# Late rows' scatters paced by the experts' products, result rows behind them, six result tiles

## The chip, the cores and the metric

One core of one Trainium2 chip. Its engines run side by side, each in the order of its own queue: PE multiplies (its products land in PSUM, in banks), DVE and ACT copy and compute, POOL here prepares and issues the indirect DMAs (scatters of rows to numbered places in DRAM), SP issues the other DMAs. They wait for each other by semaphores. The metric is the device time of the whole program in microseconds; lower is better.

## The reference, cut to what matters

```python
def reference(**kwargs):
    attn_out = _attn_ref(**attn_kwargs)            # (4, 4, 1088, 32)
    x = attn_out.transpose(0, 2, 1, 3).reshape(4352, 128)
    ...
    expert_idx = token_ids * np.int64(2654435761) % np.int64(8)
    for e in range(8):
        mask = expert_idx == e
        xe = x[mask]
        h = np.maximum(xe @ w1[e], 0.0)            # 128 -> 1024
        out[mask] = h @ w2[e]                      # 1024 -> 128
```

The attention (`_attn_ref`) is linear: features of q and k are products of two sketches, kv and z are sums over the sequence, and each of the 4352 rows of x is a quotient. All is float32.

## The kernel before, in words

**Attention.** Four batches go one after the other. Each ends in 8 blocks of 128 finished rows (`xs[b]`, b from 0 to 3); the last 64 rows of each batch are gathered in two tail tiles (`xs_tail`). A finished block is scattered to the DRAM table `x_rows`, where every expert has its own stretch: one indirect DMA of POOL per block, in `scatter_x` (line 686 in the profile). Batches 0 and 1 and the first tail are the early rows (8 + 8 + 1 scatters); they fill the experts' first 256 places. Batches 2 and 3 and the second tail are the late rows (17 scatters), which fill the places behind.

**Experts.** There are 16 groups: groups 0 to 7 are the first 256 rows of the 8 experts, groups 8 to 15 their late rows, between 313 and 278 each. A group has eight products of `layer1` (line 989, 128 of the 1024 hidden columns each, into a PSUM bank `hp`; four banks take turns), whose result ACT and DVE copy out through a ReLU in turn (`evict`, lines 774 and 776), and eight products of `layer2` (line 997, into `op`). The loop over (g, c) writes `layer1(g, c)`, then `layer2(g - 1, c)`, then what the table `beside` holds for that place. I call the place (g, c) slot 8g + c. The order on every engine is the order in which this program text is run; an instruction waits only for the data that it uses, and where `add_manual_dep` adds a wait.

**Rows in and out.** `fetch(k)` (SP, line 837) reads chunk k of `x_rows` from group k - 3 on; the chunks of groups 0 to 7 don't wait for the late rows, chunk 8 and later do. `turn_in` and `join_in` transpose it by DMA as two halves and put these together for `layer1`. On the way out, `out_columns` copies `op` as two halves (ACT), `turn_out` transposes them by two DMAs (SP, slot 8g + 1), `join_out` joins them in a tile `os` (DVE, slot 8g + 5), and `scatter_next` takes the next finished block of 128 rows and scatters it to the output (POOL, line 1000). `load_next` fetches the weights of experts 4 to 7, each load waiting for the product of its slot.

**What stands around the change.** `late_rows`, at slot 7, finishes the late rows' numbers (`sidx`, DVE) and then writes all 17 scatters, one right after the other. From group 2 on, `scatter_next` stands at c = 6, c = 7 and the next group's c = 0. `os` has three buffers, so the fourth `join_out` waits until the first tile's scatters have landed.

Of the kernel before, what the change touches and what calls it, by code (L numbers as in the profile page):

```python
# [9 lines left out]
F32 = mybir.dt.float32  # L10
# [14 lines left out]
def _half(ap, x):  # L25

    return ap.bitcast(U16).rearrange("p (n two) -> p n two", two=2)[:, :, x]
# [3 lines left out]
def kernel(  # L31
# [13 lines left out]
    P = 128  # L45
    B, H, S, D = q.shape
    R = S1.shape[0]
    N, DM = out.shape
    E, _, F = moe_w1.shape
    assert (H * D, DM, B * S, R * R * 2) == (P, P, N, P)  # L50
    T = S // P
    SM = T * P
    SP = S - SM
    TT = B // 2
# [5 lines left out]
    FC = F // P  # L60
# [6 lines left out]
    G = 2 * E  # L67
# [7 lines left out]
    XR = GE + N  # L75
    GQ = T // Q
    BIG = 1 << 30
    assert GE % P == 0 and caps[-1] >= P and ST <= P and 2 * CE == C and EB == TT


# [34 lines left out]
    def tail_col(cls):  # L115
        return cls * CE + TT * T

    def col_of(b, t):
        return b // TT * CE + b % TT * T + t
# [121 lines left out]
    G_.memset(empty_row[:], 0.0)  # L241
    G_.memset(empty_row[:, DM:DM + 1].bitcast(I32), BIG)

# [14 lines left out]
    xs = [const.tile([P, T, XW], F32, name=f"xs{b}") for b in range(B)]  # L258
    xs_tail = [const.tile([P, XW], F32, name=f"xs_tail{u}") for u in range(B // TT)]
# [218 lines left out]
    def route_blocks_end(p):  # L478
        own = spread[:].rearrange("p (n t) i -> p n t i", t=Q)
        nc.vector.tensor_tensor(own, p[:], own_t[:].unsqueeze(1).unsqueeze(3).to_broadcast([P, TT * GQ, Q, Q]), op=OP.mult)  # L480
        with nc.allow_low_precision(reason="the numbers of rows are whole"):
            to = sidx[:, main_cols(1)].rearrange("p (b i g) -> p b g i", b=TT, g=GQ)
            for b in range(TT):
                nc.vector.tensor_reduce(to[:, b], own[:, b * GQ:(b + 1) * GQ].rearrange("p g t i -> p g i t"), axis=AX.X, op=OP.add)
# [200 lines left out]
    def scatter_x(row, c):  # L685
        st_ = G_.indirect_dma_start(  # L686
            out=x_dram[:], out_offset=bass.IndirectOffsetOnAxis(ap=sidx[:, c:c + 1], axis=0),
            in_=row, in_offset=None, bounds_check=E * XR, oob_is_err=False)
        tc.declare_no_dep(st_.ins, group="x_rows", reason="distinct rows")
        tc.add_to_no_dep_group("x_rows", st_.ins)  # L690
        if c >= CE:
            tc.declare_no_dep(st_.ins, group="early_loads", reason="rows of late slots")
            tc.add_to_no_dep_group("late_rows", st_.ins)

    def x_tail(u, fT, psum=x_bank):
        p = x_tail_products(u, fT, ms[u * TT:(u + 1) * TT], psum)
        den = const.tile([P, 1, H], F32, tag="den_tail", name="den_tail", bufs=1)
        dens_of(den, [p], [(0, 1)])
        nc.vector.reciprocal(den[:], den[:])
        over_dens(xs_tail[u][:, 0:DM].unsqueeze(1), p, den[:], 1)  # L700

    def scatter_tail(u):
        scatter_x(xs_tail[u][:], tail_col(u))


    def side_turned(src):
# [74 lines left out]
    def first_of(g):  # L781
        if g <= E:
            return g * GE
        return E * GE + sum(caps[:g - E]) + (GAP if g >= G - 1 else 0)
# [25 lines left out]
    CT = 3  # L810
# [166 lines left out]
    moe = ctx.enter_context(tc.tile_pool(name="moe", bufs=3))  # L977
# [4 lines left out]
    last_mm = [None]  # L982
# [70 lines left out]

    def join_out():
        i, n, tts = turned_out.pop()
        os = moe.tile([P, CT, DM], F32, tag="os", name="os", bufs=3)
        for x in range(2):
            nc.vector.tensor_copy(_half(os[:].rearrange("p a b -> p (a b)"), x)[:, 0:n * DM],  # L1058
                                  tts[x][:, 0:n].rearrange("p a b -> p (a b)"))
        ready.extend((os[:, j], put[:, i + j:i + j + 1]) for j in range(n))  # L1060

    def out_rows(i, n):
        tp = ps_x.tile([P, CT, P], F32, tag="x", name="tp")
        for j in range(n):
            nc.tensor.transpose(tp[:, j], late_cols[:, (i + j) * P - LATE:(i + j + 1) * P - LATE], ident[:])
        os = moe.tile([P, CT, DM], F32, tag="os", name="os", bufs=3)
        for j in range(n):
            nc.vector.tensor_copy(os[:, j], tp[:, j])
        ready.extend((os[:, j], put[:, i + j:i + j + 1]) for j in range(n))
# [10 lines left out]
    def overflow_tables():  # L1080
        nc.vector.tensor_scalar(few[:], free_to[:, 1, E - 1:E], float(P), None, op0=OP.is_le)
        nc.vector.tensor_scalar(begin[:], place[:], -float(GD), float(GL + GE), op0=OP.mult, op1=OP.add)
        yield
        nc.vector.tensor_tensor(begin[:], begin[:], few[:].to_broadcast([P, E]), op=OP.mult)
        nc.vector.tensor_tensor(nt[:], left[:], begin[:], op=OP.subtract)
        yield
        nc.vector.tensor_scalar(nt[:], nt[:], float(GE + P - 1), 0.0, op0=OP.add, op1=OP.max)
        nc.vector.tensor_copy(nt_i[:], nt[:])
        yield
        nc.vector.tensor_scalar(nt_i[:], nt_i[:], P.bit_length() - 1, None, op0=OP.logical_shift_right)  # L1090
        nc.vector.tensor_copy(nt[:], nt_i[:])
        yield
        nc.vector.tensor_tensor_scan(ends[:], ones[:, 0:E], nt[:], 0.0, op0=OP.mult, op1=OP.add)
        nc.vector.tensor_copy(n_over[:], ends[:, E - 1:E])
# [4 lines left out]
    def at(g, c, f, *a):  # L1099
        beside.setdefault((g, c), []).append(lambda: f(*a))  # L1100

    def slot(n):
        return n // FC, n % FC
# [2 lines left out]

    def late_rows():
        route_blocks_end(route_blocks(bank))
        for b in range(TT, B):
            for t in range(T):  # L1110
                scatter_x(xs[b][:, t], col_of(b, t))
        scatter_tail(1)

    at(0, 7, late_rows)


    for k in range(4, G):
# [20 lines left out]
    for g in range(2, G - 1):  # L1138
        at(g, 1, turn_out, first_of(g - 1) // P)
        at(g, 5, join_out)  # L1140
        for c in (6, 7):
            at(g, c, scatter_next)
        at(g + 1, 0, scatter_next)
        if g == G - 4:

            at(g, 7, nc.gpsimd.drain)
        if g == G - 3:
            at(g + 1, 0, nc.gpsimd.drain)
    tables = overflow_tables()
    for i in range(5):  # L1150
        at(G - 5 + i // 4, 2 * (i % 4), next, tables, None)
# [13 lines left out]
    g, lo = G - 1, size_of(G - 1) - P  # L1165
# [26 lines left out]
    op = ps_o.tile([P, DM], F32, tag="o", name="op_rows")  # L1192
    for c in range(FC):
        nc.tensor.matmul(op[:], hTs[g][:, c, lo:lo + P], w2[:, g % E, c], start=(c == 0), stop=(c == FC - 1))
    os = moe.tile([P, CT, DM], F32, tag="os", name="os", bufs=3)
    nc.scalar.copy(os[:, 0], op[:])
    scatter(os[:, 0], put[:, ST - 1:ST])
    ordered.close()
# [7 lines left out]
    with tc.If(turns > 0):  # L1206
        nc.gpsimd.drain()
        with tc.For_i(0, turns):
# [15 lines left out]
            at = moe.tile([P, 6], F32, tag="at", name="at", bufs=1)  # L1224
# [46 lines left out]
            op = ps_o.tile([P, DM], F32, tag="o", name="op")  # L1271
            for c in range(FC):
                nc.tensor.matmul(op[:], hr[:, c], wo[1][:, c * P:(c + 1) * P], start=(c == 0), stop=(c == FC - 1))
            os = moe.tile([P, CT, DM], F32, tag="os", name="os", bufs=3)
            nc.scalar.copy(os[:, 0], op[:])
            scatter(os[:, 0], put1[:])

# [29 lines left out]
```

## Time and profile before

| | |
|---|---|
| median of 3 runs | 211.09 us (211.08 to 211.7) |
| the profiled execution | 210.28 us |
| its span, first to last instruction | 208.6 us |
| PE busy | 181.0 us (87%) |
| DVE, ACT, POOL busy | 90.8, 66.0, 81.5 us |
| scatters of POOL | 35 to `x_rows`, 35 to the output, about 0.98 us each |

The page's second part divides the span into 40 slices of 5.2 us and gives each engine's busy share there in tenths; PEclk is the granted clock of PE in tenths of 2.4 GHz. A row of a timeline has the start, the time, engine and line, the operation with its tiles, and in brackets how long the engine stood idle before it and what ended that; "issue" and "remote" mean that the profile shows nothing it waited for.

### The profile page before, as it was taken

How to read it: one execution, taken by the hardware profiler on the slowest of the kernel's cores; microseconds unless marked ns; L12 is line 12 of the kernel's file. 1: busy time of each engine (PE TensorE's matmuls, PEld its weight loads, DVE VectorE, ACT ScalarE, POOL GpSimd, SP SyncE). 2: the span in 40 equal slices, each digit the busy share in tenths (PEclk: the TensorE clock that was granted, in tenths of full speed). 3: DMA queues.
4: the chain of work that ended last, by engine and by line, in shares of the span. 5: the costliest groups of instructions: out<-in, count | busy, mean ns of one | idle time of the engine just before them, and what ended most of it. 6: DMA issues, size and time to landing. Idle time of an engine off the chain costs nothing. (4 is left out here: it accounts for less than half of the span.)

```text
span 208.6 us, 4037 instructions
## 1 busy us (share of the span) xinstructions
PE 181.0 (87%) x1459; PEld 142.0 (68%) x1459; DVE 90.8 (44%) x287; ACT 66.0 (32%) x176; POOL 81.5 (39%) x128
## 2 busy tenths in 40 slices
PE   8999839945988998137999999999999999999981
PEld 2769329725947886025888888877777777777970
DVE  3785536627455640003144426444525635424320
ACT  2587604420542721003133233313223132231220
POOL 7755751472010177771132133033213123054742
PEclk9999955995899999955799999999999999999999
DMA  4999999310019469312555495844153142150100
GB/s 121 272 344 294 318 303 337 85 57 31 3 47 272 127 171 210 95 57 81 134 165 148 99 176 149 94 91 101 43 104 72 38 106 71 27 91 25 38 30 28
DMA packets 43524, 26.35 MB, mean 126 GB/s; under 512 B 21913, under 2 KB 41370, under 8 KB 43503
## 3 DMA queue, kind: packets, MB, share of 16 engines
q1 hardware_dynamic: 40383, 21.14, 40.3%
q0 software_dynamic: 2304, 4.78, 8.4%
q8 instruction: 12, 0.20, 0.4%
q10 hardware_dynamic: 816, 0.17, 0.4%
q14 instruction: 9, 0.07, 0.1%
HBM read 17.42 MB, written 4.95 MB: 107 GB/s over the span
## 5 line engine op out<-in xcount | busy, mean ns | idle before, releaser
L997 PE MATMUL op<-hT,w 128*128 128x256 f32 (+8 forms) x256 | 78.2, 397 | 0.0
L1000 POOL DMA_INDIRECT out_dram<-os,put x35 | 34.6, 989 | 77.8 <-DVE os L1058 61.7
L776 DVE TENSOR_SCALAR hT<-hp 128x256 f32<-128x256 f32 (+9 forms) x64 | 27.4, 428 | 77.4 <-PE hp L989 50.6
L997 PEld LDWEIGHTS op<-hT,w 128*128 128x128 f32 x256 | 48.8, 195 | 11.2
L774 ACT ACTIVATE hT<-hp 128x256 f32<-128x256 f32 (+9 forms) x72 | 27.9, 390 | 78.4 <-PE hp L989 59.2
L989 PE MATMUL hp<-xT,w 128*128 128x256 f32 x128 | 40.1, 404 | 9.7 <-issue 8.3
L989 PE MATMUL hp<-xT_late,w 128*128 128x313 f32 (+8 forms) x144 | 41.9, 386 | 0.0
L686 POOL DMA_INDIRECT x_rows<-xs,sidx x32 | 31.5, 983 | 21.5 <-issue 8.5
L989 PEld LDWEIGHTS hp<-xT,w 128*128 128x128 f32 x128 | 24.9, 200 | 15.4 <-issue 9.9
L989 PEld LDWEIGHTS hp<-xT_late,w 128*128 128x128 f32 x144 | 25.3, 189 | 7.0 <-issue 0.3
L622 PE MATMUL kv<-va,kp 128*64 128x33 f32 x256 | 12.9, 247 | 9.6 <-issue 9.4
L622 PEld LDWEIGHTS kv<-va,kp 128*64 128x64 f32 x256 | 11.6, 165 | 13.7 <-issue 11.9
L560 DVE TENSOR_TENSOR fT<-q_first,each_ps 128x512 f32<-128x512 f32 x16 | 10.4, 684 | 14.3 <-remote 11.7
L544 PE MATMUL each_ps<-qT,s_each 32*64 32x512 f32 x128 | 12.4, 609 | 1.1 <-ACT q_first L556 0.7
L556 ACT COPY q_first<-each_ps 128x512 f32<-128x512 f32 x16 | 8.9, 593 | 4.4 <-PE each_ps L544 3.6
L644 PE MATMUL x_ps<-m,fT 128*64 128x66 f32 x256 | 9.0, 230 | 0.5 <-ACT m L631 0.5
L644 PEld LDWEIGHTS x_ps<-m,fT 128*64 128x64 f32 x256 | 8.4, 144 | 1.3 <-ACT m L631 0.6
L865 DVE COPY xh<-xg 128x256 uint16<-128x256 uint16 (+1 forms) x28 | 8.4, 340 | 0.0
L631 ACT COPY m<-kv 64x66 f32<-64x66 f32 x8 | 1.7, 209 | 19.8 <-PE kv L622 19.8
L544 PEld LDWEIGHTS each_ps<-qT,s_each 32*64 32x64 f32 x128 | 3.9, 130 | 5.8 <-ACT q_first L556 3.0
L1037 ACT COPY half<-op 128x256 uint16<-128x256 uint16 x16 | 5.2, 377 | 6.5 <-PE op L997 5.5
L1058 DVE COPY os<-turned 128x256 uint16<-128x256 uint16 (+1 forms) x26 | 6.8, 311 | 0.6 <-DMA turned<-half 0.6
(170 smaller groups left out, 138.3 us busy)
## 6 DMA issues: line engine op xcount, KB each, us to landing
w<-in_moe_w_dram SPq DMA_DIRECT2D x16, 512.0 KB
q<-in_q_dram SPq DMA_DIRECT2D x4, 512.0 KB
v<-in_v_dram SPq DMA_DIRECT2D x4, 512.0 KB
xg<-x_rows SPq DMA_DIRECT2D x12, 129.0 KB
k<-in_k_dram SPq DMA_DIRECT2D x3, 512.0 KB
out_dram<-os,put POOLq DMA_INDIRECT x35
x_rows<-xs,sidx POOLq DMA_INDIRECT x32
k<-in_k_dram SPq DMA_DIRECT2D x3, 128.0 KB
```

The lines of the kernel that those rows point to most:

```text
L544: nc.tensor.matmul(p[HALVES[x]], s_each[rows, a].rearrange("p i j -> p (i j)"), src_of(rows, x), start=True, stop=True, skip_group_check=True)
L556: nc.scalar.copy(firsts[:, t], ps[t][:])
L560: nc.vector.tensor_tensor(fT[:, t * GQ:(t + 1) * GQ], firsts[:, t], ps[t][:], op=OP.mult)
L622: nc.tensor.matmul(kv[HALVES[x], z], f[:, x], w[:, x], start=(n == 0 and z == 0), stop=(n == T), skip_group_check=True)
L644: nc.tensor.matmul(p[x, j, z], fT[:, t0 + j, z, x], m[:, z], start=True, stop=True, skip_group_check=True)
L686: st_ = G_.indirect_dma_start(out=x_dram[:], out_offset=bass.IndirectOffsetOnAxis(ap=sidx[:, c:c + 1], axis=0), in_=row, in_offset=None, b ...
L774: nc.scalar.activation(dst, src, AF.Relu if relu else AF.Copy)
L776: return nc.vector.tensor_scalar(dst, src, 0.0, None, op0=OP.max).ins
L865: nc.vector.tensor_copy(xh[:, x * w:(x + 1) * w].rearrange("p (a b) -> p a b", a=n), xg3[k][:, 0:n].bitcast(U16).rearrange("p a (b two) -> ...
L989: last_mm[0] = nc.tensor.matmul(hp[:, 0:hi - lo], w1[:, g % E, c * P:(c + 1) * P], x_columns(first_of(g) + lo, first_of(g) + hi), start=Tr ...
L997: nc.tensor.matmul(ops[g][:, 0:hi - lo], w2[:, g % E, c], hTs[g][:, c, lo:hi], start=(c == 0), stop=(c == FC - 1))
L1000: st_ = nc.gpsimd.indirect_dma_start(out=out[:], out_offset=bass.IndirectOffsetOnAxis(ap=idx, axis=0), in_=src, in_offset=None, bounds_che ...
```

## The change

`late_rows` now only prepares the 17 scatters. `late_next` writes one of them, and makes it wait for the layer1 product of the slot in which it stands (`beside_now`); it stands at slots 7, 9, 11, ..., 39. `scatter_next` no longer stands three times per group: it stands at every second slot from 41 to 119, and takes a block if one is finished in program order. It waits for no product. `os` gets six buffers.

```diff
+    OS = 6
...
-        os = moe.tile([P, CT, DM], F32, tag="os", name="os", bufs=3)
+        os = moe.tile([P, CT, DM], F32, tag="os", name="os", bufs=OS)
...
     def late_rows():
         route_blocks_end(route_blocks(bank))
-        for b in range(TT, B):
-            for t in range(T):
-                scatter_x(xs[b][:, t], col_of(b, t))
-        scatter_tail(1)
-
-    at(0, 7, late_rows)
+        late_rows_left.extend(lambda b=b, t=t: scatter_x(xs[b][:, t], col_of(b, t)) for b in range(TT, B) for t in range(T))
+        late_rows_left.append(lambda: scatter_tail(1))
+
+    late_rows_left = []
+
+    def beside_now(ins):
+        tc.add_manual_dep(ins, last_mm[0].ins.name,
+                          mybir.DependencyInfo(mybir.DependencyClass.Sync, mybir.DependencyReason.DATA), reason="pace")
+
+    def late_next():
+        beside_now(late_rows_left.pop(0)().ins)
+
+    LATE_AT = 7
+    at(*slot(LATE_AT), late_rows)
+    for i in range(2 * T + 1):
+        at(*slot(LATE_AT + 2 * i), late_next)
+    OUT_AT = LATE_AT + 2 * (2 * T + 1)
...
-        for c in (6, 7):
-            at(g, c, scatter_next)
-        at(g + 1, 0, scatter_next)
...
+    for i in range(OUT_AT, (G - 1) * FC, 2):
+        at(*slot(i), scatter_next)
```

The orders on PE and ACT are as they were, and so is SP's. On POOL the scatters keep their sequence; what differs is what they wait for. Here are the first late scatters on POOL before, in slot 7 (`xs2` is the tile of batch 2, `sidx` the row numbers; DMASW0 to DMASW7 are the semaphores of POOL's DMAs, used in turn, so that each scatter waits for the one eight before it; PE and DVE are those engines' own):

```order
L1021 MEMSET late_cols_1125 128x68 [waits DMAHW2_49,DMAHW3_49,DMAHW1_49,DMAHW5_49,DMAHW0_49,DMAHW6_49,DVE_49,DMAHW7_49,PE_49,Pool_49]
L686 DMA x_rows<-xs2_187,sidx_224 36993x144 [waits DMASW4_49,DVE_49]
L686 DMA x_rows<-xs2_187,sidx_224 36993x144 [waits DMASW5_49]
L686 DMA x_rows<-xs2_187,sidx_224 36993x144 [waits DMASW6_49]
L686 DMA x_rows<-xs2_187,sidx_224 36993x144 [waits DMASW7_49]
```

And the same place after:

```order
L1023 MEMSET late_cols_1125 128x68 [waits DMAHW2_49,DMAHW3_49,DMAHW1_49,DMAHW5_49,DMAHW0_49,DMAHW6_49,DVE_49,DMAHW7_49,PE_49,Pool_49]
L687 DMA x_rows<-xs2_187,sidx_224 36993x144 [waits DMASW4_49,DVE_49,PE_49]
L687 DMA x_rows<-xs2_187,sidx_224 36993x144 [waits DMASW5_49,PE_49]
L687 DMA x_rows<-xs2_187,sidx_224 36993x144 [waits DMASW6_49,PE_49]
L687 DMA x_rows<-xs2_187,sidx_224 36993x144 [waits DMASW7_49,PE_49]
```

Each late scatter has got a wait for PE, and nothing else has moved. The next place on POOL is the end of the late rows and the first result rows; before, the last four late scatters (`xs3`, `xs_tail1`) stand back to back in slot 7, the result rows in groups 2 to 4:

```order
L686 DMA x_rows<-xs3_188,sidx_224 36993x144 [waits DMASW1_49]
L686 DMA x_rows<-xs3_188,sidx_224 36993x144 [waits DMASW2_49]
L686 DMA x_rows<-xs3_188,sidx_224 36993x144 [waits DMASW3_49]
L686 DMA x_rows<-xs_tail1_190,sidx_224 36993x144 [waits DMASW4_49]
L1000 DMA out_0_dram<-os_1319,put_225 4352x128 [waits DMASW5_49,DVE_49]
L1000 DMA out_0_dram<-os_1319,put_225 4352x128 [waits DMASW6_49]
L1000 DMA out_0_dram<-os_1383,put_225 4352x128 [waits DMASW7_49,DVE_49]
L1000 DMA out_0_dram<-os_1383,put_225 4352x128 [waits DMASW0_49]
L1000 DMA out_0_dram<-os_1445,put_225 4352x128 [waits DMASW1_49,DVE_49]
L1000 DMA out_0_dram<-os_1445,put_225 4352x128 [waits DMASW2_49]
```

After, with the late scatters at slots 33 to 39 and the result rows from slot 41 on:

```order
L687 DMA x_rows<-xs3_188,sidx_224 36993x144 [waits DMASW1_49,PE_49]
L687 DMA x_rows<-xs3_188,sidx_224 36993x144 [waits DMASW2_49,PE_49]
L687 DMA x_rows<-xs3_188,sidx_224 36993x144 [waits DMASW3_49,PE_49]
L687 DMA x_rows<-xs_tail1_190,sidx_224 36993x144 [waits DMASW4_49,PE_49]
L1002 DMA out_0_dram<-os_1292,put_225 4352x128 [waits DMASW5_49,DVE_49]
L1002 DMA out_0_dram<-os_1292,put_225 4352x128 [waits DMASW6_49]
L1002 DMA out_0_dram<-os_1362,put_225 4352x128 [waits DMASW7_49,DVE_49]
L1002 DMA out_0_dram<-os_1362,put_225 4352x128 [waits DMASW0_49]
L1002 DMA out_0_dram<-os_1430,put_225 4352x128 [waits DMASW1_49,DVE_49]
L1002 DMA out_0_dram<-os_1430,put_225 4352x128 [waits DMASW2_49]
```

The late ones wait for a product of PE; the result rows behind them wait for DVE's copies into their `os` tile and for no product, though they now stand from slot 41 on. The third place is DVE at the fourth `join_out` (slot 45), before:

```order
L776 TENSOR_SCALAR hT_1470<-hp_1492 128x256 [waits PE_49]
L776 TENSOR_SCALAR hT_1470<-hp_1504 128x256 [waits PE_49]
L872 COPY xT_1508<-xh_turned_1454 128x256 [waits DMAHW1_49]
L872 COPY xT_1508<-xh_turned_1454 128x256
L1058 COPY os_1511<-turned0_1480 128x256 [waits DMAHW2_49,DMASW6_49,DMASW5_49]
L1058 COPY os_1511<-turned1_1482 128x256 [waits DMAHW3_49]
L846 COPY put_225<-xg3_1428 128x2 [waits DMAHW7_49]
```

And after:

```order
L778 TENSOR_SCALAR hT_1452<-hp_1477 128x256 [waits PE_49]
L778 TENSOR_SCALAR hT_1452<-hp_1492 128x256 [waits PE_49]
L874 COPY xT_1496<-xh_turned_1439 128x256 [waits DMAHW1_49]
L874 COPY xT_1496<-xh_turned_1439 128x256
L1060 COPY os_1499<-turned0_1462 128x256 [waits DMAHW2_49]
L1060 COPY os_1499<-turned1_1464 128x256 [waits DMAHW3_49]
L848 COPY put_225<-xg3_1407 128x2 [waits DMAHW7_49]
```

The copy into the fourth `os` tile no longer waits for the two scatters (DMASW6, DMASW5) that empty the first tile.

## Rows read from the trace of the kernel before

**Rows 1.** The page: the span, and the busy share of PE in 40 slices of 5.2 us with its granted clock.

```profile
span 208.6 us, 4037 instructions
...
PE   8999839945988998137999999999999999999981
...
PEclk9999955995899999955799999999999999999999
```

**Rows 2.** The timeline of PE alone from 70 to 112 us: the layer1 products of slots 17 to 27 (the second of group 2 to the fourth of group 3); the rows left out between them are layer2's.

```profile
78.77 0.59 PE L989 MATMUL hp<-xT,w 128*128 128x256 f32 x2
...
79.64 0.59 PE L989 MATMUL hp<-xT,w 128*128 128x256 f32 x2
...
80.50 0.59 PE L989 MATMUL hp<-xT,w 128*128 128x256 f32 x2
...
81.36 0.59 PE L989 MATMUL hp<-xT,w 128*128 128x256 f32 x2
...
83.24 0.70 PE L989 MATMUL hp<-xT,w 128*128 128x256 f32 x2 [0.85 <-issue]
...
88.98 1.22 PE L989 MATMUL hp<-xT,w 128*128 128x256 f32 x2 [4.61 <-issue]
...
93.94 1.22 PE L989 MATMUL hp<-xT,w 128*128 128x256 f32 x2 [2.88 <-issue]
...
97.32 1.19 PE L989 MATMUL hp<-xT,w 128*128 128x256 f32 x2 [1.30 <-ACT half L1037]
...
99.16 1.06 PE L989 MATMUL hp<-xT,w 128*128 128x256 f32 x2
...
100.87 1.06 PE L989 MATMUL hp<-xT,w 128*128 128x256 f32 x2
...
102.20 0.59 PE L989 MATMUL hp<-xT,w 128*128 128x256 f32 x2
```

**Rows 3.** Busy time of the engines in three stretches: from and to, length, busy us and instructions of PE, PEld, DVE, ACT and POOL, granted clock, mean share of the 16 DMA engines, GB/s.

```profile
78.40:82.40 4.00, 3.99 (x19) 3.16 (x17) 0.00 (x0) 0.78 (x3) 3.08 (x4) 1.00 1.16 226
82.40:102.20 19.80, 10.16 (x25) 6.99 (x25) 3.31 (x12) 2.20 (x7) 10.56 (x11) 0.66 0.36 97
102.20:130.00 27.80, 27.80 (x130) 24.38 (x129) 12.52 (x44) 8.50 (x25) 7.97 (x8) 1.00 0.59 140
```

**Rows 4.** The timeline of ACT alone: its copies out of layer1's banks at slots 18 and 20 (the second row with slot 22 as well).

```profile
88.55 0.38 ACT L774 ACTIVATE hT<-hp 128x256 f32<-128x256 f32 x1 [9.15 <-remote]
96.29 0.66 ACT L774 ACTIVATE hT<-hp 128x256 f32<-128x256 f32 x2 [7.36 <-PE op L997]
```

**Rows 5.** The timeline of DVE alone: its copies out of the banks of slots 17, 19 and 21, then the first and the last of a block of copies once a group, the last being that of the next bank.

```profile
82.76 0.43 DVE L776 TENSOR_SCALAR hT<-hp 128x256 f32<-128x256 f32 x1 [4.66 <-PE op L997]
93.47 0.42 DVE L776 TENSOR_SCALAR hT<-hp 128x256 f32<-128x256 f32 x1 [10.28 <-issue]
96.37 0.43 DVE L776 TENSOR_SCALAR hT<-hp 128x256 f32<-128x256 f32 x1 [2.48 <-PE op L997]
96.72 0.50 DVE L872 COPY xT<-xh_turned 128x256 uint16<-128x256 uint16 x2
...
97.99 0.41 DVE L776 TENSOR_SCALAR hT<-hp 128x256 f32<-128x256 f32 x1
```

**Rows 6.** The timeline of POOL alone: the first and the last of the 17 late scatters.

```profile
71.89 0.98 POOL L686 DMA_INDIRECT x_rows<-xs,sidx  x1 [8.32 <-DVE sidx L484]
...
92.42 0.98 POOL L686 DMA_INDIRECT x_rows<-xs_tail,sidx  x1 [0.30 <-issue]
```

**Rows 7.** The same for the early rows: the first scatter of the first run of eight, the first of the second run of eight, and the first tail's scatter.

```profile
19.30 1.11 POOL L686 DMA_INDIRECT x_rows<-xs,sidx  x1 [1.48 <-DVE xs L663]
...
38.71 0.97 POOL L686 DMA_INDIRECT x_rows<-xs,sidx  x1 [2.91 <-DVE xs L663]
...
58.12 0.98 POOL L686 DMA_INDIRECT x_rows<-xs_tail,sidx  x1 [9.46 <-DVE xs_tail L663]
```

**Rows 8.** The timeline of PE alone in the attention: the rows from which on its products of kv follow each other without a gap again.

```profile
30.74 2.39 PE L622 MATMUL kv<-va,kp 128*64 128x33 f32 x41 [1.07 <-issue]
...
50.08 1.94 PE L622 MATMUL kv<-va,kp 128*64 128x33 f32 x32 [0.51 <-issue]
```

**Rows 9.** Busy time in three more stretches, columns as in rows 3: the two runs of eight, and 14 us of the experts with two pairs of result rows.

```profile
19.30:30.80 11.50, 7.01 (x74) 4.49 (x73) 5.69 (x10) 4.62 (x9) 7.99 (x8) 0.82 1.02 307
38.70:50.10 11.40, 6.38 (x81) 3.80 (x78) 5.35 (x10) 3.55 (x7) 7.82 (x8) 0.87 0.16 53
103.00:117.00 14.00, 14.00 (x67) 12.26 (x66) 6.14 (x23) 4.17 (x12) 4.01 (x4) 1.00 0.54 146
```

**Rows 10.** The timeline of SP's queue: the fetches of the first four chunks, a load of weights, the transposes of `turn_in` and `turn_out`, and the fetch of chunk 8.

```profile
60.63 1.91 SPq L837 DMA_DIRECT2D xg<-x_rows  x4
...
78.95 0.01 SPq L176 DMA_DIRECT2D w<-in_moe_w_dram  x1
79.69 0.81 SPq L867 DMA_TRANSPOSE xh_turned<-xh  x1
81.22 2.81 SPq L1050 DMA_TRANSPOSE turned<-half  x2
...
117.28 1.09 SPq L837 DMA_DIRECT2D xg<-x_rows  x3
```

More of the change, by code (lines that the diff above doesn't have):

```diff
@@ L693, in scatter_x @@
             tc.add_to_no_dep_group("late_rows", st_.ins)
+        return st_
     def x_tail(u, fT, psum=x_bank):
@@ L702, in scatter_tail @@
     def scatter_tail(u):
-        scatter_x(xs_tail[u][:], tail_col(u))
+        return scatter_x(xs_tail[u][:], tail_col(u))
     def side_turned(src):
@@ L1065, in out_rows @@
             nc.tensor.transpose(tp[:, j], late_cols[:, (i + j) * P - LATE:(i + j + 1) * P - LATE], ident[:])
-        os = moe.tile([P, CT, DM], F32, tag="os", name="os", bufs=3)
+        os = moe.tile([P, CT, DM], F32, tag="os", name="os", bufs=OS)
         for j in range(n):
@@ L1194 @@
         nc.tensor.matmul(op[:], hTs[g][:, c, lo:lo + P], w2[:, g % E, c], start=(c == 0), stop=(c == FC - 1))
-    os = moe.tile([P, CT, DM], F32, tag="os", name="os", bufs=3)
+    os = moe.tile([P, CT, DM], F32, tag="os", name="os", bufs=OS)
     nc.scalar.copy(os[:, 0], op[:])
@@ L1273 @@
                 nc.tensor.matmul(op[:], hr[:, c], wo[1][:, c * P:(c + 1) * P], start=(c == 0), stop=(c == FC - 1))
-            os = moe.tile([P, CT, DM], F32, tag="os", name="os", bufs=3)
+            os = moe.tile([P, CT, DM], F32, tag="os", name="os", bufs=OS)
             nc.scalar.copy(os[:, 0], op[:])
```

## The prediction

> **What bounds the kernel now.** I read the page first [rows 1]: PE is at nine tenths or more of almost every slice of the experts' half, except slices 17 to 19 (about 83 to 99 us), where it falls to 1, 3 and 7 tenths and its clock to half. Then the timeline of PE through that hole [rows 2]. I count slots: slot n is the n-th product of layer1, eight to a group, from group 1 on with one product of layer2 behind it; slot 17 is the second of group 2. Slots 17 to 20 start at 78.77, 79.64, 80.50 and 81.36, so a slot takes (81.36 - 78.77)/3 = 0.863 us. Slots 21, 22, 23 and 24 start at 83.24, 88.98, 93.94 and 97.32, slots 24 to 26 at half clock (about 1.71 us each), and from slot 27 (102.20) the pace is regular again. At the regular pace slot 27 would have started at 81.36 + 7 x 0.863 = 87.40. **The hole costs 102.20 - 87.40 = 14.8 us.** Behind it PE is busy 27.80 of 27.80 us [rows 3], so what is lost there is lost at the end.
>
> What is PE waiting for? Its four hp banks. Slot 21 needs the bank of slot 17, which DVE empties at 82.76 (0.43 us, and PE starts at 83.24); slot 22 needs that of slot 18, emptied by ACT at 88.55 (PE: 88.98); slot 23 that of slot 19, by DVE at 93.47 (PE: 93.94) [rows 2, 4, 5]. And ACT and DVE? They stand idle for 9.15 and 10.28 us in front of these copies, although the products were issued at 79.64 and 80.50. The products are long done; the word of it arrives late. At 96.29 and 96.37 both come free at once.
>
> What ends there? POOL's run of 17 late scatters, begun at 71.89 and issued every (92.42 - 71.89)/16 = 1.28 us [rows 6]. The two earlier runs of eight show the same: they begin at 19.30 and 38.71 [rows 7], PE crawls in pieces that wait for nothing the profile shows, and full speed is back at 30.74 and 50.08 [rows 8]. Per scatter, from the run's start to the release: (30.74 - 19.30)/8 = 1.43, (50.08 - 38.71)/8 = 1.42, (96.29 - 71.89)/17 = 1.435. Three runs of different length give one figure: behind POOL something serves a scatter in about 1.43 us, POOL feeds it one every 1.28, and while it is behind, PE's messages pass only now and then. Pairs of scatters do no harm: from 103 to 117, four scatters in two pairs, PE 14.00 of 14.00 [rows 9].
>
> **The change, part by part.** *Late rows spaced out.* The 17 scatters come at slots 7, 9, ... 39 and each waits for that slot's layer1 product. Two slots are 1.73 us, more than 1.43, so nothing builds up, with 0.30 us to spare per scatter. The first few are still fed every 1.28 us (the first cannot start before its row numbers, 71.89 now; by then slots 7 and 9 are issued), which is four scatters and no more. So the hole goes: -14.8 us. The wait feeds back the right way: if PE's word is late, the next scatter is late too. What is left is that one scatter may hold a message back for up to 1.43 us. A bank is needed again four slots later, 3.45 us, less 0.59 for the product and 0.43 for the copy: 2.4 us to spare; DVE's block of copies once a group (96.72 to 97.99 [rows 5]) eats 1.3 of it. I take 0.5 us for the whole stretch, between 0 and 2. Behind the waiting scatter on POOL stand only scatters. The waits cost no instruction on PE, whose order is untouched.
>
> *Late rows end later.* Slot 39 falls at 78.77 + 22 x 0.863 = 97.8; its product takes 0.59, so the last late scatter starts at about 98.3 instead of 92.42. The tail's scatter at 58.12 let the fetch behind it go at 60.63 [rows 7, 10], so issue to landing is 2.5 us: 100.8. Its first reader is the fetch of chunk 8 on SP at slot 42 (100.3). SP has two transposes of turn_out ahead of it at slot 41 (2.81 us for the pair at 81.22), so that it would not come before about 102.4 anyway; today it comes at 117.28, 2.1 us behind its slot [rows 10]. Cost 0. If that cover were gone, 0.5 us of SP would shift, with ten slots before group 7 needs what is queued behind it.
>
> The Trainium skill, "DMA: Bandwidth & Descriptors", section "Rules for kernel authors", speaks against this move: issue a DMA early and wait on its semaphore late. By that rule these scatters were best where they were; the landing above says that the last one still has 1.6 us in hand, so by the rule too the sum would lose nothing here.
>
> *Result rows behind them.* Now they go two per group from group 2 on, as soon as joined. After the change the first stands behind the last late scatter, and it waits for its os tile alone, not for PE. By then three os tiles (joined at slots 21, 29, 37) are full, six scatters, and the fourth (slot 45, about 102.9) is full before POOL gets to it at 98.3 + 7 x 1.28 = 107.3. So POOL issues nine in a row: the last late one and eight results. The fifth tile (slot 53, about 109.8, its copies a microsecond later) makes a pause. By 1.43 us per scatter the messages are free at 98.3 + 9 x 1.43 = 111.2. **This is the new wait.** Lower bound: nothing, since the experts' own run held PE up only from 82.4 on, 10.5 us after its start, and nine scatters last 12.9: 2.4 us. Upper bound: in the runs of eight PE idled 11.50 - 7.01 = 4.5 and 11.40 - 6.38 = 5.0 us [rows 9]; nine give 5.6, and if the clock falls behind that (it was 0.82 and 0.87 there), five slots at half clock, as many as in the hole (22 to 26), add 5 x 0.85 = 4.3: 9.9. The nearest row is that of the experts' own stretch; I take 3.
>
> *Six buffers.* Slot 45's join no longer waits for the first tile's two scatters; without the three more buffers it would wait for them to land at about 103.4, half a microsecond. Worth 0 beside the above. The last part of the kernel keeps its scatters.
>
> Sum: -14.8 + 0.5 + 3 = -11.3. The profiled execution took 210.28 us (span 208.6 and 1.7 around it), so 199.0; the median of the runs is 0.8 higher, so **199.8 us**.
>
> **The rivals.** *The result rows cost nothing* (nine scatters are too few to stop four banks): -14.8 to -13.3, about 197. For it: the 10.5 us of grace above. Against: the runs of eight. *They cost all they can*, with the clock: -14.8 + 0.5 + 5.6 to 9.9, about 202 to 207, in the middle 204.5. For it: both runs of eight lowered the clock. Against: PE's products were then small and far fewer.
>
> *The scatters are not the cause.* At 78.95 SP issues a load of weights, then three transposes [rows 10], and the DMA share is 1.16 from 78.4 to 82.4 [rows 3], just before the first late copy. If that holds PE up, the hole stays and so does the time, 211.1. Against: from 38.7 to 50.1 the share was 0.16 and PE idled all the same, and from 103 to 117 loads and transposes ran without harm [rows 9]. The Trainium skill, same page, section "Issuing engines are not separate DMA queues", says that DMAs of all issuers end on the same 16 engines and interleave; by that alone spreading them moves no work and the time stays 211.1. The 0.36 share in the hole [rows 3] says that these engines were not full.
>
> *Slower: single scatters are enough.* Each scatter may hold PE's messages for its own 1.43 of 1.73 us, DVE's block of copies takes the rest of the slack, PE waits a little in every slot and its clock falls to 1.2 GHz for the whole paced stretch, where a slot takes 1.71 instead of 0.863 us. For all 33 slots that is 27.9 us against the 14.8 saved: 211.1 + 13.1 = 224. It decides from 14.8/0.85 = 17 slots on. Against: at 1.71 us per slot a scatter comes every 3.4 us and the cause is gone; and in the present run PE still issued regularly at 81.36, 9.5 us in.
>
> **How the numbers follow.** Forecast 0.47; result rows free 0.25; result rows at full price 0.18; not the cause 0.04; slower 0.06. The range takes the first two whole and the near half of the third: 195.8 (all of the 14.8, and half a microsecond for the runs' own spread) to 205.5. About 0.3% is what a measurement of this kernel tells from no change: faster 0.90, within 0.3% 0.04, slower 0.06.
>
> **What would show it.** After: layer1 products 0.86 us apart from slot 17 to slot 38, x_rows scatters 1.73 us apart from the fifth on, no copy of ACT or DVE with more than 3 us of idle in front before about 103. A run of nine scatters from about 98, the last eight to out_dram, and any idle of PE between 103 and 112 released at its start + 9 x 1.43. The forecast is wrong if PE is regular through 112 (too slow by 3), if its clock falls there (too fast), or if copies come late while scatters are 1.73 us apart (the cause is misread). The fetch of chunk 8 should go at about 102.4 and wait for no x_rows.

## The result, and the profile after

| | before | after |
|---|---|---|
| median of 4 runs each | 211.17 us (211.08 to 211.7) | 201.81 us (201.36 to 204.26) |
| ratio, 95% interval | | 0.9575 (0.9496 to 0.9655): faster |
| the profiled execution, its span | 210.28, 208.6 us | 201.49, 199.6 us |

The forecast was 199.8 us, range 195.8 to 205.5. Single executions of one kernel lie up to 6 us apart (198.71 to 204.95 us for e4b_three_buffers below), so below I rest on stretches of a trace where I can, and on medians only for larger differences; ratios leave disturbed executions out, and so aren't always the quotient of the medians.

Four parts of the profile after answer to rows of before. First the page, as in [rows 1]:

```profile
span 199.6 us, 4046 instructions
...
PE   8989937982988999999998599999999999999970
...
PEclk9999995897599999999999799999999999999997
```

The 1, 3 and 7 of slices 17 to 19 are gone, and a new dip to 5 stands in slice 23 (about 110 to 115 us), with the clock at 7 in it. Next the timeline of PE, the products of layer1 at slots 9, 23, 24, 49, 50, 51, 52 and 54, which answers to [rows 2]:

```profile
72.20 0.59 PE L991 MATMUL hp<-xT,w 128*128 128x256 f32 x2
...
84.30 0.59 PE L991 MATMUL hp<-xT,w 128*128 128x256 f32 x2
...
85.40 0.67 PE L991 MATMUL hp<-xT,w 128*128 128x256 f32 x2
...
107.06 0.59 PE L991 MATMUL hp<-xT,w 128*128 128x256 f32 x2
...
108.46 0.70 PE L991 MATMUL hp<-xT,w 128*128 128x256 f32 x2 [0.37 <-ACT hT L776]
...
111.47 0.73 PE L991 MATMUL hp<-xT,w 128*128 128x256 f32 x2 [1.88 <-issue]
...
113.39 1.22 PE L991 MATMUL hp<-xT,w 128*128 128x256 f32 x2 [0.34 <-ACT hT L776]
...
116.21 0.59 PE L991 MATMUL hp<-xT,w 128*128 128x256 f32 x2
```

From slot 9 to slot 23 there are 14 slots in 84.30 - 72.20 = 12.10 us, 0.864 each. Slot 24 is (85.40 - 84.30) - 0.86 = 0.24 us late, and then all is regular up to slot 49. Slot 54 would come at 107.06 + 5 x 0.8635 = 111.38; it comes at 116.21. **The new loss is 4.83 us**: 2.59 us of idle in three gaps, the rest products at the lower clock (1.22 us for a pair at slot 52) and short waits. What ends it stands in the timelines of POOL, ACT and DVE (the first two rows are the first and the last late scatter, the next two the first and the last result row of the run; then two copies of ACT and one of DVE), for [rows 4 to 6]:

```profile
72.71 0.98 POOL L687 DMA_INDIRECT x_rows<-xs,sidx  x1 [8.79 <-PE op L999]
...
99.30 0.98 POOL L687 DMA_INDIRECT x_rows<-xs_tail,sidx  x1 [0.57 <-PE hp L991]
100.58 0.98 POOL L1002 DMA_INDIRECT out_dram<-os,put  x1 [0.30 <-issue]
...
109.79 0.98 POOL L1002 DMA_INDIRECT out_dram<-os,put  x1 [0.30 <-issue]
```

```profile
108.02 0.39 ACT L776 ACTIVATE hT<-hp 128x256 f32<-128x256 f32 x1 [4.26 <-PE hp L991]
112.41 0.65 ACT L1039 COPY half<-op 128x256 uint16<-128x256 uint16 x2 [4.00 <-PE hp L991]
```

```profile
110.99 0.42 DVE L778 TENSOR_SCALAR hT<-hp 128x256 f32<-128x256 f32 x1 [5.05 <-PE op L999]
```

The run is nine scatters, as predicted: the last late one and eight result rows, 1.28 us apart. ACT and DVE stand idle for 4 to 5 us in front of copies whose products PE has issued long before, and come free at 110.99 (DVE) and 112.41 (ACT). Start plus nine times 1.43 is 99.30 + 12.87 = 112.2. The windows say the same (columns as in [rows 3]), and SP's queue has the fetch of chunk 8 at 103.67 in place of 117.28 [rows 10]:

```profile
72.70:104.00 31.30, 31.23 (x145) 27.09 (x144) 12.93 (x47) 9.23 (x26) 19.60 (x20) 1.00 0.77 181
104.00:113.00 9.00, 6.75 (x27) 4.71 (x26) 2.56 (x11) 0.98 (x4) 5.25 (x6) 0.94 0.52 140
```

```profile
103.67 1.44 SPq L839 DMA_DIRECT2D xg<-x_rows  x3
```

The account: -14.80 (hole) + 0.24 (paced stretch) + 4.83 (result run) + 0.34 (slot 9 at 72.20 us against 71.86, ahead of the change) = -9.39; the span went down by 9.0, so 0.4 us more is lost behind these, 0.18 of it in a gap in front of the first late product (125.19 us); the rest I have not traced.

### The profile page after: what moved, and what is told of

Same layout as the page of the kernel before. It is cut to its first block, busy times and chain, and to the rows that moved or that the text cites. A ratio compares the mean times of both kernels' runs of the same rounds, so it can differ in the third digit from the quotient of the medians.

```text
span 199.6 us, 4046 instructions
## 1 busy us (share of the span) xinstructions
PE 178.2 (89%) x1459; PEld 139.8 (70%) x1459; DVE 91.0 (46%) x287; ACT 66.1 (33%) x176; POOL 81.8 (41%) x128
## 5 line engine op out<-in xcount | busy, mean ns | idle before, releaser
L999 PE MATMUL op<-hT,w 128*128 128x256 f32 (+8 forms) x256 | 77.3, 392 | 0.0
L999 PEld LDWEIGHTS op<-hT,w 128*128 128x128 f32 x256 | 47.8, 191 | 10.7
L991 PE MATMUL hp<-xT,w 128*128 128x256 f32 x128 | 38.2, 388 | 2.8 <-issue 1.9
L991 PEld LDWEIGHTS hp<-xT,w 128*128 128x128 f32 x128 | 24.1, 193 | 8.0 <-issue 2.7
L561 DVE TENSOR_TENSOR fT<-q_first,each_ps 128x512 f32<-128x512 f32 x16 | 10.5, 684 | 16.0 <-remote 13.3
L1039 ACT COPY half<-op 128x256 uint16<-128x256 uint16 x16 | 5.2, 375 | 10.5 <-PE hp L991 4.9
L590 DVE TENSOR_TENSOR kp<-first_of_ab,abk_ps 128x1024 f32<-128x1024 f32 x5 | 6.1, 1215 | 2.2 <-ACT va L607 1.3
```

The lines of the kernel that those rows point to most:

```text
L561: nc.vector.tensor_tensor(fT[:, t * GQ:(t + 1) * GQ], firsts[:, t], ps[t][:], op=OP.mult)
L991: last_mm[0] = nc.tensor.matmul(hp[:, 0:hi - lo], w1[:, g % E, c * P:(c + 1) * P], x_columns(first_of(g) + lo, first_of(g) + hi), start=Tr ...
L999: nc.tensor.matmul(ops[g][:, 0:hi - lo], w2[:, g % E, c], hTs[g][:, c, lo:hi], start=(c == 0), stop=(c == FC - 1))
```

## The experiments

The theory: a run of POOL's scatters, fed every 1.28 us and served in about 1.43, holds back the word of PE's finished products until its start + 1.43 per scatter; scatters further apart don't. Rivals: the place of the scatters in the program, the buffers, loads and transposes of SP, or that single scatters hold PE too. Each group of runs had one chip, with the kernel before beside it; groups 3 and 5 had the same one.

| group | kernel | us, median | before there | ratio, 95% interval |
|---|---|---|---|---|
| 1 | e1_place_only | 180.67 | 179.57 | 1.0041 (0.9952 to 1.013) |
| 1 | e2_results_paced | 180.6 | 179.57 | 1.0056 (1.0006 to 1.0106) |
| 1 | e3_pace_alone | 182.24 | 179.57 | 1.0061 (0.9999 to 1.0124) |
| 1 | e4_three_buffers | 179.19 | 179.57 | 0.9973 (0.992 to 1.0027) |
| 2 | a2_after_again | 202.81 | 210.86 | 0.9524 (0.9495 to 0.9552) |
| 2 | e1b_place_only | 211.17 | 210.86 | none given |
| 2 | e2b_results_paced | 200.88 | 210.86 | 0.9559 (0.9517 to 0.9602) |
| 3 | e7_all_spaced | 195.5 | 212.48 | 0.9235 (0.914 to 0.9329) |
| 3 | e5_filler | 214.33 | 212.48 | none given |
| 4 | e8_one_memset | 199.37 | 214.13 | 0.9353 (0.9212 to 0.9493) |
| 4 | e9_late_memset | 211.3 | 214.13 | 0.994 (0.9832 to 1.0048) |
| 5 | e4b_three_buffers | 202.04 | 210.27 | 0.953 (0.9458 to 0.9602) |

**Group 1: a chip without the hole.** Four edits of the kernel after. *e1_place_only* takes the wait away:

```diff
-        beside_now(late_rows_left.pop(0)().ins)
+        late_rows_left.pop(0)()
```

> The kernel after, without the wait of the late scatters for PE's products: every instruction stands where it stands after, six buffers too, but POOL can issue the 17 late scatters as fast as it gets through them. Theory (a run of scatters fed every 1.28 us and served in about 1.43 us holds back the word of PE's finished products): the hole is back, late copies of ACT and DVE from about 82 to 96 us, and the time is 211.1 (210.5 to 214, if result rows lengthen the run). Rival, it is the place of the scatters or of the result rows in the program, or the buffers: 201.8 as after. Rival, loads of weights and transposes at 78 to 82 us make the hole: it would be gone after for no reason that this kernel lacks, so 201.8 too.

*e2_results_paced* also gives the result rows a wait (`scatter` returns its instruction):

```diff
+    def out_next():
+        if ready:
+            beside_now(scatter(*ready.pop(0)).ins)
...
-        at(*slot(i), scatter_next)
+        at(*slot(i), out_next)
```

> The kernel after, with each result row from slot 41 on also waiting for the layer1 product of its slot, so that the run of nine scatters from 99.30 us goes apart into single ones, 1.73 us from each other. Theory: the 4.8 us that PE lost between 107.06 and 116.21 come back, and nothing else moves: 197.0 (196.5 to 198). Rival, PE is held up there by something else (the fetch of chunk 8 at 103.67, its transposes): 201.8.

*e3_pace_alone* puts the result rows back to c = 6, 7, 0 and has three buffers, *e4_three_buffers* sets only `OS = 3`.

> The kernel after, with only the late rows paced: the result rows stand where they stood before (three places in each group from group 2 on) and os has three buffers. Theory: no run of nine, but in groups 2 to 4 there are four late scatters and up to two result rows per group, 6 x 1.43 = 8.6 us of service in 8 x 0.863 = 6.9 us, so the word of PE falls behind by up to 1.7 us per group and the loss is spread over these groups: 199 to 204, with no single gap as long as the 1.88 us at 111.47 after. Rival, only an unbroken run counts: 197.

> The kernel after with three os buffers in place of six. The prediction gave the buffers nothing: DVE would wait at the fourth join until the first two result rows have landed, about 103.4 us, half a microsecond behind its place, in front of a run that holds PE anyway: 201.8, within 0.7. Rival, DVE's wait ends later, since the first result rows now land in the middle of the run (100.58 + 2.5 + queue): then DVE holds the hp banks and it is 203 to 206.

None of these numbers came, since here the kernel before took 179.57 us and not 211. By the ratios all four lie within 0.7% of it, so they tell nothing about the rivals; but they tell something that the prediction had not thought of. (e3_pace_alone was not run on another chip, so its own question, whether result rows among the paced late ones do harm, stays open.) The trace of e1_place_only in this group, the first and the last late scatter on POOL, and two windows: the first run of eight in the attention, and the 17 late scatters:

```profile
58.74 0.98 POOL L687 DMA_INDIRECT x_rows<-xs,sidx  x1 [9.72 <-DVE sidx L485]
...
79.31 0.98 POOL L687 DMA_INDIRECT x_rows<-xs_tail,sidx  x1 [0.30 <-issue]
```

```profile
19.50:31.00 11.50, 11.50 (x225) 8.90 (x226) 10.98 (x31) 7.01 (x18) 8.97 (x9) 1.00 1.09 336
58.70:80.40 21.70, 21.67 (x101) 18.71 (x100) 9.46 (x35) 6.52 (x19) 16.67 (x17) 1.00 0.79 178
```

POOL feeds them every (79.31 - 58.74)/16 = 1.29 us, as in [rows 6], the share of the DMA engines is 1.09 and 0.79, and PE is busy 11.50 of 11.50 and 21.67 of 21.70 us at full clock. In [rows 9] it was 7.01 of 11.50. So the same run of the same instructions does no harm on this chip. The theory's 1.43 us is no constant of the kernel. (It is one chip in one group of runs; that it is the chip, and not something else that was different then, is not shown.)

**Group 2: the same on a chip with the hole.** The kernel after once more, and the first two edits again.

> The kernel after, unchanged, on whatever chip this is, with the kernel before timed beside it. Theory: what the pacing gives is the hole, and the hole hangs on the chip. Where the kernel before takes about 211 us, this takes 201.8 (ratio 0.957). Where the kernel before takes about 180 us, as beside the first four kernels, POOL issues the late scatters every 1.28 us too, but no copy of ACT or DVE comes late, and there is nothing to gain: 179.6 (ratio 0.995 to 1.005). Rival, the pacing by itself gives something on every chip: under 0.99 there too.

> The kernel after without the wait of the late scatters for PE's products; all else as after. On a chip where the kernel before takes about 211 us: theory (the run of scatters holds back the word of PE) the hole is back and it is 211 (210.5 to 214); rival (the place in the program, or the six buffers) 201.8. On a chip where the kernel before takes about 180 us: 180 by both.

> The kernel after with each result row from slot 41 on waiting for the product of its slot as well, which takes the run of nine scatters apart. On a chip where the kernel before takes about 211 us: theory 197.0 (196.5 to 198), the 4.8 us between 107.06 and 116.21 of the kernel after being back; rival (the stall there has another cause) 201.8. On a chip where the kernel before takes about 180 us: 180 by both.

Without the wait, the hole is back, though every scatter keeps its place after and os has six buffers. The trace of e1b_place_only, POOL's first late scatter, ACT's copies in the hole, and its window:

```profile
71.20 0.98 POOL L687 DMA_INDIRECT x_rows<-xs,sidx  x1 [8.31 <-DVE sidx L485]
```

```profile
88.39 0.38 ACT L776 ACTIVATE hT<-hp 128x256 f32<-128x256 f32 x1 [9.69 <-remote]
95.39 0.66 ACT L776 ACTIVATE hT<-hp 128x256 f32<-128x256 f32 x2 [6.62 <-PE op L999]
```

```profile
80.80:100.50 19.70, 10.26 (x27) 6.73 (x26) 3.31 (x12) 1.97 (x6) 11.16 (x12) 0.66 0.40 96
```

(95.39 - 71.20)/17 = 1.42 us per scatter, as before. Place and buffers fall as rivals for what removed the hole. In a2_after_again the result run costs more than in the first trace: here the timeline of PE, the products of slots 49 to 51 and of slot 55.

```profile
106.86 0.59 PE L991 MATMUL hp<-xT,w 128*128 128x256 f32 x2
...
109.66 0.70 PE L991 MATMUL hp<-xT,w 128*128 128x256 f32 x2 [1.77 <-issue]
...
112.55 1.22 PE L991 MATMUL hp<-xT,w 128*128 128x256 f32 x2 [1.76 <-DVE hT L778]
...
119.01 0.59 PE L991 MATMUL hp<-xT,w 128*128 128x256 f32 x2
```

119.01 - (106.86 + 6 x 0.8635) = 6.97 us, with four slots at the lower clock (1.22 to 0.91 us for a pair). The window from 104 to 113 us, in a2_after_again and, with the result rows paced, in e2b_results_paced, and the one row of PE with a gap up to 125 us in the latter:

```profile
104.00:113.00 9.00, 5.47 (x24) 4.16 (x23) 2.55 (x10) 1.27 (x5) 4.99 (x5) 0.92 0.48 139
```

```profile
104.00:113.00 9.00, 9.00 (x42) 7.59 (x41) 4.01 (x15) 2.48 (x7) 5.18 (x6) 1.00 0.94 163
```

```profile
121.00 0.77 PE L991 MATMUL hp<-xT_late,w 128*128 128x313 f32 x2 [0.85 <-DVE xT_late L874]
```

PE is busy 9.00 of 9.00 us where it was 5.47 in a2_after_again and 6.75 in the first trace: the run of nine was the cause of that stall. What comes instead is 0.85 us at the first late chunk, whose transposes are just late. The profiled execution took 197.51 us, as expected (197.0), and that of a2_after_again 202.96. But by the medians the expectation was missed: 200.88 and 202.81 are only 1.9 us apart, and the intervals of the ratios (0.9559 and 0.9524) overlap. The other executions of e2b_results_paced took 200.5 to 202.2 us at a lower mean clock, and where they lost it no trace of mine shows. So the trace shows that the stall goes; that the kernel gets faster by it is not shown.

**Groups 3 and 4: distance without a wait for PE.** *e7_all_spaced* is e2_results_paced with three memsets of POOL behind each early scatter; *e5_filler* is the kernel before with four behind each late one.

```diff
+    pad = const.tile([P, 100], F32)
...
         if c >= CE:
...
+        else:
+            for _ in range(3):
+                G_.memset(pad[:], 0.0)
```

> The kernel after, with the result rows paced by products as well, and with three small memsets of POOL behind each early scatter, so that the two runs of eight in the attention come one per about 1.64 us instead of 1.28, more than the 1.43 of their service. Theory: where the kernel before takes about 211 us, PE's gaps in the kv products go too: 4.5 + 5.0 us of idle [rows 9] and up to 6 us at half clock behind them come off the 197.5 us that the kernel with paced result rows took in its profiled execution, less up to 3 us by which the early rows land later: 185 (182 to 190). Rival, those gaps have another cause (loads, the share of the DMA engines was 1.02 in the first): 197 to 200. On a chip where the kernel before takes about 180 us: nothing to gain, and up to 3 us lost to the later landing: 179.5 to 183.

> The kernel before, with one edit: behind each late scatter POOL runs four small memsets, so that the scatters come one per about 1.76 us; nothing waits for PE, the result rows stand where they stood, three os tiles. Theory (what counts is the distance of the scatters alone): where the kernel before takes about 211 us the hole of 14.8 us goes; the late scatters then end near 102 us, and the six to eight result rows that are ready behind them make a run as in the kernel after, 4.8 us: 201 (197 to 203). Rival (the wait for PE is needed, since it feeds back): 207 to 211. On a chip where the kernel before takes about 180 us: 180 by both.

In e5_filler no scatter waits for PE, they come (114.68 - 74.67)/16 = 2.50 us apart, and the hole is gone. Its window from the first late scatter to 110 us, and the next rows of DVE and PE:

```profile
74.60:110.00 35.40, 35.40 (x165) 31.02 (x165) 14.63 (x50) 10.63 (x31) 24.95 (x71) 1.00 0.64 153
```

```profile
122.68 0.79 DVE L1061 COPY os<-turned 128x256 uint16<-128x256 uint16 x2 [15.47 <-issue]
```

```profile
124.35 1.22 PE L992 MATMUL hp<-xT,w 128*128 128x256 f32 x2 [13.27 <-DVE hT L779]
```

PE 35.40 of 35.40: distance alone does it. The time is no better: 214.33 us, and 209.88 in the quickest execution, so neither the 201 of the theory nor the rival's 207 to 211 came. In the trace this is because at this distance the late scatters end late, and the result rows behind them: DVE's next join needs the first of three os tiles back, whose two scatters go at 117.22 and 118.50 us; it waits 15.47 us, and PE with it 13.27 us for its bank. In e7_all_spaced the two windows cover the spaced early runs; then the first two scatters of the run with the memsets between, and PE's one long gap:

```profile
19.60:36.40 16.80, 16.74 (x306) 11.51 (x307) 15.09 (x38) 10.24 (x24) 12.01 (x30) 1.00 0.98 311
38.80:57.90 19.10, 11.48 (x244) 8.15 (x244) 9.17 (x19) 4.96 (x16) 13.55 (x34) 0.96 0.10 34
```

```profile
22.03 1.01 POOL L688 DMA_INDIRECT x_rows<-xs,sidx  x1 [0.56 <-issue]
23.01 0.70 POOL L698 MEMSET pad<- 128x100 f32 x3
24.27 0.98 POOL L688 DMA_INDIRECT x_rows<-xs,sidx  x1 [0.55 <-issue]
```

```profile
61.70 0.66 PE L862 MATMUL xp<-ident,xg 128*128 128x128 f32 x2 [9.52 <-DMA xg<-x_rows]
```

In the first run PE is busy 16.74 of 16.80 us, against 7.01 of 11.50 [rows 9]; the kv products run in one piece. (The second window ends in the wait that follows.) The memsets cost more than I had reckoned, 2.24 us per scatter and not 1.64, so the early rows land late and PE waits 9.52 us for their fetch. The 185 us of the theory did not come, nor the rival's 197 to 200: it took 195.5 us, the least on any chip with the hole.

*e8_one_memset* and *e9_late_memset* were to bring the distance down to 1.64 us, with one memset of 16 columns; e9 is the kernel before with that behind each late scatter and six buffers.

> The kernel with paced result rows and memsets behind the early scatters, with one memset of 16 columns in place of three of 100. In the trace of that one the gaps in the kv products were gone, but three memsets made it 2.20 us per scatter, and PE waited 9.52 us for the fetch of the early rows. One memset makes 0.98 + 0.11 + 0.55 = 1.64 us, still over 1.43; 17 scatters come 17 x 0.56 = 9.5 us earlier. Theory, where the kernel before takes about 211 us: the wait for the fetch shrinks to about a microsecond, and from 193.7 us it goes to 185 (183.5 to 188). Rival, 1.64 is too near to the service time, kv gaps come back in part: 188 to 194. On a chip where the kernel before takes about 180 us: 179.5 to 182 by both.

> The kernel before with one small memset of POOL behind each late scatter (1.64 us apart, no wait for PE) and six os buffers; the result rows stand where they stood. In the trace of the same thing with four memsets PE was regular from 74 to 110 us, but the scatters came 2.45 us apart, and DVE then waited 15.47 us for the third os buffer to come free. Theory, where the kernel before takes about 211 us: the distance alone does what the wait for PE does in the kernel after, the late scatters end near 101 us, and result rows make a run behind them: 201.8 (199 to 204). Rival, without PE's word to pace it the run falls behind: 205 to 211. On a chip where the kernel before takes about 180 us: 180 by both.

Neither did: e8 took 199.37 us (185 by the theory, 188 to 194 by the rival) and e9 211.3 (201.8, and 205 to 211). POOL's timeline of e9_late_memset shows why, and PE's what follows:

```profile
73.12 0.98 POOL L687 DMA_INDIRECT x_rows<-xs,sidx  x1 [0.18 <-issue]
74.09 0.14 POOL L695 MEMSET pad<- 128x16 f32 x1
74.41 0.98 POOL L687 DMA_INDIRECT x_rows<-xs,sidx  x1 [0.18 <-issue]
```

```profile
85.64 0.70 PE L991 MATMUL hp<-xT,w 128*128 128x256 f32 x2 [3.29 <-issue]
...
94.66 1.22 PE L991 MATMUL hp<-xT,w 128*128 128x256 f32 x2 [7.90 <-issue]
```

The memset runs inside the 0.30 us that POOL idles between scatters anyway: 74.41 - 73.12 = 1.29 us, nothing is further apart, and the hole is there with gaps of 3.29 and 7.90 us. e8 has the gaps of the kv products back as well, with 1.28 us between its early scatters. As expectations both failed; as controls they are of use. It is not the memset, and not the six buffers, but the distance that cures, and 1.29 us is too little.

**Group 5: the buffers.**

> The kernel after with three os buffers in place of six, on a chip where the kernel before takes about 211 us. In the trace of the kernel with four memsets DVE got a third os buffer back about 4.2 us after the second result row was issued. Here the second result row goes at about 101.9, so DVE would wait at its fourth join from 103.5 to about 106, and PE's banks with it, in front of a run of result rows that holds PE anyway until about 112. Prediction's value for the buffers, 0: 201.8, within 1, and a wait of DVE of 2 to 3 us in front of the fourth copy into os. Rival, the word of these landings is held back by the run like PE's: DVE waits until 112 and the late end moves with it, 205 to 208.

202.04 us, ratio 0.953 (the kernel after: 0.9575 and 0.9524). DVE's fourth join, in the copies around it:

```profile
107.40 0.43 DVE L778 TENSOR_SCALAR hT<-hp 128x256 f32<-128x256 f32 x1 [1.52 <-PE hp L991]
...
108.39 0.49 DVE L1060 COPY os<-turned 128x256 uint16<-128x256 uint16 x2
```

The join starts 0.99 us behind the copy before it; with six buffers (104.24, 104.98) it is 0.74. The wait that I expected at this place, 2 to 3 us, is a quarter of one. Three more buffers are worth nothing here that the spread of the runs (about 1.5 us either way) would let one see.

## Why the prediction was right, and where its sizes were off

**What made the hole: right, where there is a hole.** Taking away the wait alone brings it back (e1b), distance alone takes it away (e5), a memset without distance leaves it (e9). SP's loads and transposes stand in all of these, so the rival "the scatters are not the cause" falls with them. The rule that went with it, from the Trainium skill, "DMA: Bandwidth & Descriptors", section "Issuing engines are not separate DMA queues" (all issuers' DMAs run on the same 16 engines and interleave), is not contradicted by these runs, and the engines were far from full in the hole (mean share 0.36 [rows 3], 0.40 in e1b). What failed is the rival that the prediction drew from it, that spreading the scatters leaves the time at 211.1: the section says nothing of PE's word, and it is PE's wait for that word which went.

**1.43 us per scatter: right as a size where there is a hole, wrong as a reading.** e1b_place_only gives 1.42, the first run of eight in e5_filler (30.59 - 19.17)/8 = 1.43. But the prediction took it for the time in which something behind POOL serves a scatter and falls behind. The trace of the kernel before speaks against that, as far as the transfers go: in the second run of eight, and in the last eight scatters of the hole, the packets of every scatter are over 1.90 to 1.96 us after POOL starts it, so they land every 1.28 us and nothing piles up. The last one has landed at 94.33, and ACT and DVE come free only at 96.29 and 96.37. In between the DMA engines move nothing (columns as in [rows 3]):

```profile
94.40:96.20 1.80, 1.62 (x4) 0.72 (x3) 0.00 (x0) 0.00 (x0) 0.00 (x0) 0.50 0.00 0
```

In group 1 the same scatters at the same pace hold nothing up. One more thing parts the two kinds of chip: POOL's 72 DMAs (70 scatters, two loads) raise their semaphores 16 times each, 1152 times in all, and the four traces of group 1 hold records of 1106 to 1132 of these, all others only of 570 to 749. Whether the late word and the missing records have one cause, and whether recording the trace takes part in it, no run shows. What holds the word back, and why one chip keeps up, stays open. The kernel after itself was not run on that chip; the nearest to it, with three buffers, has 0.9973 there, so no gain was seen. The prediction gave no chance to a chip without the hole, so that its range held hangs on the chip that was timed: that part was luck.

**Paced stretch: 0.5 predicted, 0.24 measured.** Four scatters were fed at 1.28 us and the rest every two slots, as said. "Single scatters are enough" is refuted by 31.23 of 31.30 us. From the fifth on the scatters came 1.42 to 2.04 us apart, 1.75 on average (1.73 predicted), and no copy of ACT or DVE before 104 us had as much as 2 us of idle in front (under 3 predicted).

**Late rows' end: right.** The fetch of chunk 8 went at 103.67 (predicted 102.4) and nothing waited for it long: the first product of late rows (125.19 us) has a gap of 0.18 us. The rule of the Trainium skill against the move (same page, "Rules for kernel authors": issue a DMA early, wait for it late) cost nothing by its own measure; issuing early is what brings the hole where there is one, 211.17 us for e1b_place_only against 202.81 for the kernel after in group 2 (209.05 and 202.96 in the profiled executions).

**Result rows behind them: the right wait, a size too small.** The run of nine is as worked out, its start (98.3 predicted, 99.30 measured) and its end too (111.2 predicted; DVE came free at 110.99, ACT at 112.41). The term was put at 3 us, because the experts' own run had left PE 10.5 us of grace; it measured 4.83, and 6.97 in the second trace. The term that was sized wrong is this one, by the choice of that row: the runs of eight, with 4.5 and 5.0 us of idle, were the nearer one, and the clock that falls behind them belongs into the likeliest value, not only into the upper bound. The interval 0 to 9.9 held both. (Its upper end counted five slots at half clock from the hole; by [rows 2] slots 24 to 26 there took 1.84, 1.71 and 1.33 us, not 1.71 each, which changes neither the 14.8 nor the sum.)

**Six buffers: 0, right.** e4b shows it, within its spread. In e5_filler, where the result rows went late, the join waited 15.47 us for the third tile and PE 13.27 us behind it; what six buffers would have saved there was not run.

**The early runs** the prediction used only as evidence. They were the larger part of what was left: PE idles 4.5 and 5.0 us in them [rows 9], before and after alike, and in the trace of e7 the kv products have no such gaps, with 9.5 us of a new wait instead. What that is worth is not settled by the times: e7's ratio is 0.9235, and that of e8, whose early runs stayed as they were, 0.9353 on another chip, with intervals that overlap. Something between 1.29 and 2.24 us per scatter would be worth a try there; it wasn't tried.

## What to carry to other kernels

When PE waits in pieces for nothing that the profile shows, and ACT and DVE idle in front of products that are long done, look for a run of indirect DMAs on POOL and divide the time from its start to the release by their number; if that is more than the distance at which they are issued, put them further apart, and check in the timeline that they really are. Ask of every run that is cut up which instructions stand behind it and form the next one. And time both kernels on more than one chip before a gain of this kind is believed: here it was 4 to 5% where the kernel before takes about 211 us, and nothing was seen to gain where it takes 180.

## What the runs showed of the hardware that was not expected

The kernel before took 179.57 us on one chip and 210 to 214 on the others. In e1_place_only, whose late scatters come every 1.29 us on the first chip and every 1.28 on another, the difference is PE's waiting during runs of scatters (21.67 of 21.70 us busy on the one; 10.26 of 19.70 in the hole on the other).

In the hole ACT and DVE came free about 2 us after the last scatter of the run had landed (94.33 to 96.29), with the DMA engines idle in between. On the chips with the hole the traces hold 570 to 749 of the 1152 rises of POOL's DMA semaphores, on the one without it 1106 to 1132.

A memset of 0.14 us between two indirect DMAs of POOL cost nothing that shows (1.29 us from one to the next, 1.28 without it), three of 100 columns cost 0.96 (2.24 in place of 1.28).
